# Weights loaded as fp32 in the same DMA row as q, k and v and cast by GpSimd, and batch 0 in another order, in a retention layer with a cosine-gated MLP

## The chip, the cores and the metric

The kernel runs on one core of a Trainium2 chip. The metric is device time in microseconds, the median of several runs of the whole program. A separate execution is profiled; all lines of traces are from it.

## What is computed

Inputs are q, k and v, each 8 batches x 8 heads x 576 positions x 64 (fp32), w_in (512 x 2048) and w_out (2048 x 512), fp32 too. The reference, cut to what matters:

```python
def _attn_ref(q, k, v):
    scores = scale * np.matmul(q, k.transpose(0, 1, 3, 2))
    gamma = 1.0 - 2.0 ** (-5.0 - np.arange(H, dtype=np.float32))
    Dmat = np.where(rel >= 0, gamma[:, None, None] ** rel[None, :, :], 0.0)   # rel = row - column
    return np.matmul(scores * Dmat[None], v)
...
x = np.ascontiguousarray(attn_out.transpose(0, 2, 1, 3)).reshape(B * S, H * D)
h = x @ w_in
g = h * np.cos(h)
return g @ w_out
```

So it is causal attention without softmax and with a decay per head, and then an MLP of width 2048 on 4608 tokens, gated by the cosine of its own hidden values.

## The kernel before

**Retention.** Positions are taken in chunks of 128. q is scaled by gamma to the position, v by gamma to minus the position (`decay`, L371), so that inside a chunk only a mask of zeros and ones is left. `scores` makes k^T q of a chunk for all heads (PSUM, names `sc` or `mm`), and VectorE masks it into `rt`. `rest` adds past and own part of a chunk's output into a PSUM bank (`po` or `mm`): four matmuls with the state `sb` of the chunks before, eight with `rt` and the scaled v (`vb`). Its result is copied to `xt`, the transposed input of the MLP. `state_mm` adds k^T v of a chunk to the running state (`st` in PSUM), and `state_copy` copies that to `sb` in two instructions of ScalarE.

Batches 0 and 1 are done chunk by chunk. Of each, k and q of the first 512 positions come as four "quads" (`quad`, L322: rows of 4 positions of one head, pieces of 1 KB), are cast or scaled (`quad_cast`), transposed on TensorE (`quad_turn`) into `kqt`, and k is transposed back (`back`) into `kq`. The v of a chunk comes in pieces of 256 bytes (`load`, L299). The last 64 positions, chunk 4, are loaded the same way. From token 1152 on there are 27 groups of 128 tokens (g = 9 to 35), loaded by `load_g` (L305), scaled by GpSimd (`casts_g`) and transposed by a DMA on SP's queue (`turn_dma`, L388 to L390, writes `kqt`); `quarters` does their retention.

**MLP.** Tokens go in tiles of 512 (j = 0 to 8). `mlp1` makes one of 16 column groups of the hidden layer: four matmuls with `win` into a bank, a cosine on ScalarE (a sine with a shift, `cb`, L552), a product on VectorE (`gt`, L554). For j = 0 the 512 tokens of batch 0 are taken in two halves of 256 for the first four groups, (0, 256) from chunks 0 and 1 and (256, 256) from chunks 2 and 3. The product with `wout` is done plainly for j = 0 and 1 (`plain2`, four matmuls a step; for j = 0 step n takes the n//4-th quarter of w_out) and by a scheme of seven products after that, for which VectorE makes sums of w_out's blocks (`tsum`).

**Order.** Everything is emitted by one Python program (`emit`, L905) that puts each instruction behind the one before on its engine; waits come from a small scheduler that knows who wrote and read each buffer. Loads of q, k and v go to 16 fp32 buffers `ld` of 128 x 512 in turn (`fetch`, L285) by SP's DMA queue. They stand in a list, `pend`; `pump` (L883) issues from its front as many as have a buffer whose reader has been emitted, and holds groups back while too many buffers are in use. SP does its row in order, DMA transposes among it, each with the waits for its own buffer.

**The weights** come by DMAs that GpSimd issues (`w_in_load`, L327, and `w_out_load`, L332): eight, each a quarter of a matrix (1 MB of fp32), which the DMA itself casts to bf16 in `win` or `wout`. In GpSimd's row w_in's four stand between the scalings of batch 0's v, w_out's four behind them. An entry `after` in the list lets SP wait for the second piece of w_in before it fetches anything for batch 0's last chunk and batch 1.

Of the kernel before, what the change touches and what calls it, by code (L numbers as in the profile page):

```python
# [12 lines left out]
DFF = 2048  # L13
DM = H_ * D_
# [39 lines left out]
class Tok:  # L54
    __slots__ = ("eng", "sem", "val", "clock", "seq")
    n = 0
# [87 lines left out]
class _Kernel:  # L144
# [182 lines left out]
    def w_in_load(self, g):  # L327
        dst = bass.AP(self.WIN, 512 * g, [[4 * DFF, 128], [DFF, 4], [1, 512]])
        src = bass.AP(self.w_in, 512 * g, [[DFF, 128], [128 * DFF, 4], [1, 512]])
        self.wtok[f"wi{g}"] = self.s.dma("pool", f"wi{g}", lambda e: e.dma_start(dst, src), writes=[self.bWIN[g]])  # L330

    def w_out_load(self, g):  # L332
        dst = bass.AP(self.WOUT, 4 * g * DM, [[16 * DM, 128], [DM, 4], [1, DM]])
        src = bass.AP(self.w_out, 4 * g * 128 * DM, [[DM, 128], [128 * DM, 4], [1, DM]])
        w = Buf()
        t = self.s.dma("pool", f"wo{g}", lambda e: e.dma_start(dst, src), writes=[w])
        for i in range(4 * g, 4 * g + 4):
            self.bWOUT[i].w = [t]
        self.wtok[f"wo{g}"] = t
# [543 lines left out]
    def pump(self):  # L883

        while self.pend:
            fn, a = self.pend[0]
            if fn == self.after:
                if a[0] not in self.wtok:
                    return
            else:  # L890
                n = 3 if fn == self.load_g or fn == self.load and len(a) == 2 else 1
# [13 lines left out]
    def emit(self):  # L905
# [3 lines left out]
        for b in range(2):  # L909
            if b:  # L910
                self.push(self.after, "wi1")
                self.push(self.load, 0, 4)
            for c in range(NP):
                for x in "kq":
                    self.push(self.quad, x, b, c)
            for r in range(4):
                self.push(self.load, b, r, "v")
        self.push(self.load, 1, 4)
# [24 lines left out]
        for r in range(4):  # L943
            self.w_out_load(r)
# [21 lines left out]
        m1(range(2), (0, 256))  # L966
        self.rest(0, 3, state=False)
        m1(range(2, 4), (0, 256))
# [7 lines left out]
        self.casts(0, 4)  # L976
        self.pump()
# [9 lines left out]
        for n in range(16):  # L987
# [119 lines left out]
```

## Time and profile before

| | us |
|---|---|
| median of 3 runs (298.09 to 298.13) | 298.09 |
| profiled execution, its own time | 299.12 |
| span of its instructions | 297.4 |
| TensorE busy | 285.3 |
| VectorE busy | 214.6 |
| ScalarE busy | 173.9 |
| GpSimd busy | 95.6 |

HBM was read for 36.70 MB and written for 9.44 MB. The granted TensorE clock was 1.00 all through. Times in traces count from the start of the span. In a timeline a row gives start, length, engine, line, operation, output<-input, shape and count, and in brackets the idle time of the engine ahead of it and what ended that; SPq is SP's DMA queue. "Busy" of TensorE includes the pipelining of matmuls, and a few matmul records are missing, so that "x2" stands for three here and there. In the chain of waits each row is a piece of the chain that ended last: start, length, who.

### The profile page before, as it was taken

To read this page: it belongs to the slowest core of one execution; us is meant where nothing else is said; L and a number is where in the kernel's file an instruction comes from. 1 tells how busy PE (TensorE), PEld (TensorE's weight loads), DVE (VectorE), ACT (ScalarE), POOL (GpSimd) and SP (SyncE) were. 2 spreads that over 40 slices of the span, in tenths; PEclk is the share of its full clock that TensorE was granted. 3 is DMA by queue.
4 is the path that set the end of the run, shared out by engine and by line. 5 is a ranking of instruction groups with operands and counts; after the bars stand their busy time and mean duration, and the time that the engine had idled before them with its cause. 6 is when DMAs were issued, how large, how long until landed. Compare 5 with 4: busy or idle time off the path is not lost.

```text
span 297.4 us, 8336 instructions
## 1 busy us (share of the span) xinstructions
PE 285.3 (96%) x3526; PEld 180.6 (61%) x3558; DVE 214.6 (72%) x465; ACT 173.9 (58%) x344; POOL 95.6 (32%) x120
## 2 busy tenths in 40 slices
PE   6899999999998999999999999999999999999996
PEld 2465455655553568646864785478547854785485
DVE  3667848568567688579857985798579757956973
ACT  6688624797347664566457535753586358535720
POOL 3580237754426430580058006700670030000000
PEclk9999999999999999999999999999999999999999
DMA  6999999999999999999999965899591170013013
GB/s 202 230 200 193 197 330 182 270 228 181 210 227 236 186 202 215 251 203 182 207 237 224 197 150 145 174 228 166 153 200 5 37 143 3 2 36 108 0 37 106
DMA packets 142325, 49.70 MB, mean 167 GB/s; under 512 B 125904, under 2 KB 141264, under 8 KB 142288
## 3 DMA queue, kind: packets, MB, share of 16 engines
q1 hardware_dynamic: 129280, 35.53, 67.3%
q10 hardware_dynamic: 8784, 9.44, 9.9%
q0 software_dynamic: 4224, 4.19, 8.7%
q8 instruction: 28, 0.46, 0.7%
q14 instruction: 9, 0.07, 0.1%
HBM read 36.70 MB, written 9.44 MB: 155 GB/s over the span
## 4 chain that ended last, share of the span: by engine, by line
PE 84%; DMA 9%; issue 2%; SPq 2%; DVE 1%; ACT 1%; DVEq 0%
PE mm L461 56%; PE mm L463 19%; DMA ld<-in_q_dram 3%; PE st L709 3%; PE sc L709 2%; DMA win<-in_moe_w_in_dram 2%; DMA ld<-in_v_dram 2%; DMA kqt<-kq 2%; SPq L290 2%; PE po L709 2%; PE sc L461 1%; PE po L461 1%; PE st L461 0%; PE sc L463 0%; ACT cb L552 0%
## 5 line engine op out<-in xcount | busy, mean ns | idle before, releaser
L554 DVE TENSOR_TENSOR gt<-mm,cb 128x512 bf16<-128x512 f32 (+3 forms) x156 | 99.4, 647 | 35.0 <-ACT cb L552 34.0
L552 ACT ACTIVATE cb<-mm,c_pih 128x512 bf16<-128x512 f32 (+3 forms) x156 | 100.7, 654 | 37.3 <-PE mm L463 36.4
L461 PE MATMUL mm<-xt,win 128*128 128x512 bf16 (+3 forms) x446 | 113.4, 362 | 3.1 <-issue 1.9
L461 PEld LDWEIGHTS mm<-xt,win 128*128 128x128 bf16 x468 | 43.5, 98 | 45.2 <-DVE gt L554 0.8
L463 PE MATMUL mm<-xt,win 128*128 128x512 bf16 (+3 forms) x156 | 56.6, 363 | 0.1
L342 POOL CAST kq<-ld 128x512 bf16<-128x512 f32 (+1 forms) x29 | 17.7, 610 | 117.4 <-PE mm L463 100.6
L461 PE MATMUL mm<-wout,gt 128*128 128x256 bf16 (+1 forms) x256 | 49.1, 309 | 1.0 <-issue 0.8
L461 PE MATMUL mm<-ts,ss 128*128 128x256 bf16 x240 | 35.4, 273 | 0.0
L461 PEld LDWEIGHTS mm<-wout,gt 128*128 128x128 bf16 x264 | 24.7, 98 | 11.8 <-DVE gt L554 0.5
L342 ACT ACTIVATE u<-mm 128x512 f32<-128x512 f32 x21 | 12.5, 597 | 32.3 <-PE mm L463 32.3
L365 POOL TENSOR_TENSOR vb<-ld,wv 128x512 bf16<-128x512 f32 x27 | 28.4, 1052 | 6.4 <-DMA ld<-in_v_dram 4.0
L361 POOL TENSOR_TENSOR kq<-ld,uq 128x512 bf16<-128x512 f32 x27 | 28.2, 1044 | 4.3 <-DMA ld<-in_q_dram 4.3
L342 ACT ACTIVATE xt<-po 128x256 bf16<-128x256 f32 (+1 forms) x35 | 14.6, 418 | 23.0 <-PE st L709 15.7
L463 PE MATMUL mm<-wout,gt 128*128 128x256 bf16 (+1 forms) x88 | 27.4, 311 | 0.1
L643 DVE TENSOR_TENSOR osb<-mm,u 128x512 f32<-128x512 f32 x20 | 13.8, 688 | 18.8 <-PE mm L463 11.2
L750 DVE TENSOR_TENSOR rt<-sc,mh 128x256 bf16<-128x256 f32 x54 | 21.2, 416 | 5.9 <-PE st L709 2.5
L463 PEld LDWEIGHTS mm<-xt,win 128*128 128x128 bf16 x156 | 15.3, 98 | 16.0
L461 PEld LDWEIGHTS mm<-ts,ss 128*128 128x128 bf16 x240 | 23.0, 98 | 2.8
L463 PE MATMUL mm<-ts,ss 128*128 128x256 bf16 x80 | 21.8, 272 | 0.0
L576 DVE TENSOR_TENSOR ss<-gt 128x512 bf16<-128x512 bf16 x56 | 20.7, 417 | 0.0
L760 DVE TENSOR_TENSOR pf<-sc,pf 128x256 f32<-128x256 f32 x42 | 17.6, 420 | 1.1
L709 PE MATMUL po<-rt,vb 64*64 64x64 bf16 x216 | 13.4, 202 | 0.1
(154 smaller groups left out, 386.6 us busy)
## 6 DMA issues: line engine op xcount, KB each, us to landing
out_dram<-osb ACTq DMA_DIRECT2D x35, 256.0 KB, 3.5
ld<-in_k_dram SPq DMA_DIRECT2D x32, 256.0 KB, 4.8
ld<-in_q_dram SPq DMA_DIRECT2D x32, 256.0 KB, 5.1
ld<-in_v_dram SPq DMA_DIRECT2D x32, 256.0 KB, 5.7
win<-in_moe_w_in_dram POOLq DMA_DIRECT2D x4, 512.0 KB, 10.2
wout<-in_moe_w_out_dram POOLq DMA_DIRECT2D x4, 512.0 KB, 17.0
ld<-in_k_dram SPq DMA_DIRECT2D x8, 128.0 KB, 4.5
ld<-in_q_dram SPq DMA_DIRECT2D x8, 128.0 KB, 4.0
```

The lines of the kernel that those rows point to most:

```text
L342: fn = (lambda e: e.activation(o, x, AF.Copy)) if eng == "act" else (lambda e: e.tensor_copy(o, x))
L361: self.s.op("pool", lambda e: e.tensor_tensor(o, a, w, ALU.mult), reads=[bt, self.bUQ], writes=[self.bQB[i]])
L365: self.s.op("pool", lambda e: e.tensor_tensor(o2, a2, w2, ALU.mult), reads=[bt, self.bWV], writes=[self.bVB[i]])
L461: self.nc.tensor.matmul(o, a, b, **kw)
L463: return s.done("pe", self.nc.tensor.matmul(o, a, b, **kw), reads, writes)
L552: s.op("act", lambda e: e.activation(ci, mi, AF.Sin, bias=self.C_PIH.ap(), scale=1.0), reads=[bm, self.bC], writes=[self.bCB[i]])
L554: s.op("dve", lambda e: e.tensor_tensor(bass.AP(self.GT, dt * TB + o0, [[16 * TB, 128], [1, n]]), mi, ci, ALU.mult), reads=[bm, self.bCB[i ...
L576: self.s.op("dve", lambda e: e.tensor_tensor(self.s_(k, d), a, b, op), reads=rd, writes=[S[k - 1][p]])
L643: self.s.op("dve", lambda e: e.tensor_tensor(o, m, x, ALU.add), reads=[bm, self.bU[u]], writes=[self.bOSB[i]])
L709: inst = self.nc.tensor.matmul(o, a, c, **kw)
L750: s.op("dve", lambda e: e.tensor_tensor(bass.AP(self.RT[n % 2][x], 0, p3), bass.AP(self.SC[x], 0, p3), bass.AP(self.MH, 0, [[64, 128], [0, ...
L760: s.op("dve", lambda e: e.tensor_tensor(self.PF[t].ap(), u, self.PF[1 - t].ap(), ALU.add), reads=[self.bSU[t], self.bPF[1 - t]], writes=[s ...
```

## The change

1. The weights are fetched by SP as fp32, into the same 16 buffers as q, k and v: 32 fetches of 128 x 512 (256 KB, rows of 2 KB), four to a piece (`w_load`). GpSimd casts each into `win` or `wout` (`w_cast`, 32 instructions). GpSimd issues no DMA any more, and SP's wait for w_in's second piece is gone.
2. The list has w_in's first piece ahead of batch 0's fourth v, the other three and two pieces of w_out behind it, and w_out's last two around batch 1's quads.
3. Batch 0 is emitted in another order: chunk 1's output earlier and copied by ScalarE instead of VectorE, the first MLP groups ahead of chunk 2's state and output, the fourth v scaled by VectorE instead of GpSimd, and two pairs of idle matmuls (which only fill waits) left out.

The core of the diff:

```diff
+    def w_load(self, x, g):
+        for c in range(4):
+            if x == "in":
+                src = bass.AP(self.w_in, 128 * c * DFF + 512 * g, [[DFF, 128], [1, 512]])
+            else:
+                src = bass.AP(self.w_out, (4 * g + c) * 128 * DM, [[DM, 128], [1, DM]])
+            self.fetch((x, g, c), src, [[1, DM]], 128)
+
+    def w_cast(self, eng, x, g, cs=range(4)):
+        for c in cs:
+            t, bt = self.use((x, g, c))
...
+            u = self.copy(eng, o, t.ap(), [bt], [Buf()])
+            (self.bWIN[g] if x == "in" else self.bWOUT[4 * g + c]).w.append(u)
...
+        quads(0)
+        vs(0, range(3))
+        ws("in", [0])
+        vs(0, [3])
+        ws("in", range(1, 4))
+        ws("out", range(2))
+        self.push(self.load, 0, 4)
+        ws("out", [2])
+        quads(1)
+        ws("out", [3])
+        vs(1, range(4))
         self.push(self.load, 1, 4)
...
-        self.s.need("pool", [self.wtok["v", 0, 0]])
-        self.w_in_load(0)
         self.decay("dve", "v", 0, 0)
-        self.w_in_load(1)
-        for r in range(1, 4):
+        for r in range(1, 3):
             self.decay("pool", "v", 0, r)
-            if r < 3:
-                self.w_in_load(r + 1)
-        for r in range(4):
-            self.w_out_load(r)
+        self.w_cast("pool", "in", 0)
...
         self.scores(0, 2)
+        self.rest(0, 1, self.bank(), state=False)
         self.back(0, 2, "act")
-        self.idle(2)
         self.state_mm(0, 1)
-        self.rest(0, 1, self.bank(), "dve", False)
         self.state_copy(1)
         self.scores(0, 3, False)
-        self.idle(2)
+        self.decay("dve", "v", 0, 3)
+        m1(range(2), (0, 256))
+        for g in range(1, 4):
+            self.w_cast("pool", "in", g)
+            self.pump()
+        for g in range(2):
+            self.w_cast("pool", "out", g)
+            self.pump()
         self.state_mm(0, 2)
         self.state_copy(2)
         self.rest(0, 2, state=False)
-        m1(range(2), (0, 256))
-        self.rest(0, 3, state=False)
-        m1(range(2, 4), (0, 256))
+        m1(range(2, 3), (0, 256))
+        self.rest(0, 3, self.bank(), state=False)
+        m1(range(3, 4), (0, 256))
         m1(range(3), (256, 256))
...
         self.casts(0, 4)
+        self.w_cast("pool", "out", 2)
...
+            if n == 9:
+                self.w_cast("pool", "out", 3)
+                self.pump()
```

Three places in the rows of the engines. First SP's DMA row behind batch 0's quads, before the change (128x8x64 is a v of 128 positions, 64x8x64 a chunk 4, 128x2x256 a quad):

```order
L290 DMA ld<-in_v_dram 128x8x64 x4
L290 DMA ld<-in_k_dram 64x8x64
L290 DMA ld<-in_q_dram 64x8x64
L290 DMA ld<-in_v_dram 64x8x64
L290 DMA ld<-in_k_dram 128x2x256
L290 DMA ld<-in_q_dram 128x2x256
```

and of the change, from the same place:

```order
L290 DMA ld<-in_v_dram 128x8x64 x3
L290 DMA ld<-in_moe_w_in_dram 128x512 x4
L290 DMA ld<-in_v_dram 128x8x64
L290 DMA ld<-in_moe_w_in_dram 128x512 x12
L290 DMA ld<-in_moe_w_out_dram 128x512 x8
L290 DMA ld<-in_k_dram 64x8x64
L290 DMA ld<-in_q_dram 64x8x64
L290 DMA ld<-in_v_dram 64x8x64
L290 DMA ld<-in_moe_w_out_dram 128x512 x4
L290 DMA ld<-in_k_dram 128x2x256
```

The weights' 32 fetches, of which the last four stand behind batch 1's quads, are now in one row with the rest; from batch 1's v on, the row has the same loads and transposes in the same order as before.

Second, GpSimd behind batch 0's four casts of k, before the change:

```order
L330 DMA win<-in_moe_w_in_dram 128x4x512 x2
L378 TENSOR_TENSOR vb<-ld,wv 128x512
L330 DMA win<-in_moe_w_in_dram 128x4x512
L378 TENSOR_TENSOR vb<-ld,wv 128x512
L330 DMA win<-in_moe_w_in_dram 128x4x512
L378 TENSOR_TENSOR vb<-ld,wv 128x512
L336 DMA wout<-in_moe_w_out_dram 128x4x512 x4
L342 COPY kq<-ld 64x512
```

and of the change (the copies into win and wout are the casts):

```order
L381 TENSOR_TENSOR vb<-ld,wv 128x512 x2
L345 COPY win<-ld 128x512 x16
L345 COPY wout<-ld 128x512 x8
L345 COPY kq<-ld 64x512
L381 TENSOR_TENSOR kq<-ld,uq 64x512
L381 TENSOR_TENSOR vb<-ld,wv 64x512
L345 COPY wout<-ld 128x512 x4
L345 COPY qs<-ld 128x2x4x64 x4
L345 COPY wout<-ld 128x512 x4
```

The issues of weight DMAs ahead of the v are gone, the fourth v too, and the casts stand ahead of batch 0's chunk 4, of batch 1's quads and of batch 1's v.

Third, ScalarE from batch 0's first state copies (sb) to the cosines (cb) of the second 256 tokens, before the change:

```order
L342 ACTIVATE sb<-st 64x4x64 x2
L342 ACTIVATE xt<-po 128x4x128
L342 ACTIVATE kq<-mm 128x512
L342 ACTIVATE sb<-st 64x4x64 x4
L342 ACTIVATE xt<-po 128x4x128
L552 ACTIVATE cb<-mm,c_pih 128x256 x2
L342 ACTIVATE xt<-po 128x4x128
L552 ACTIVATE cb<-mm,c_pih 128x256 x5
```

and of the change:

```order
L345 ACTIVATE sb<-st 64x4x64 x2
L345 ACTIVATE xt<-po 128x4x128
L345 ACTIVATE xt<-mm 128x4x128
L345 ACTIVATE kq<-mm 128x512
L345 ACTIVATE sb<-st 64x4x64 x2
L555 ACTIVATE cb<-mm,c_pih 128x256 x2
L345 ACTIVATE sb<-st 64x4x64 x2
L345 ACTIVATE xt<-po 128x4x128
L555 ACTIVATE cb<-mm,c_pih 128x256
L345 ACTIVATE xt<-mm 128x4x128
L555 ACTIVATE cb<-mm,c_pih 128x256 x4
```

Chunk 1's output (xt<-mm) has come to ScalarE, and the third pair of state copies and chunk 2's output now stand behind the first two cosines.

More of the change, by code (lines that the diff above doesn't have):

```diff
@@ L325, in quad @@
         self.fetch((x, b, "c", c), src, [[4 * D_, 2], [1, 4 * D_]], 128)
[L327 to L339, printed above, removed]
+    def w_load(self, x, g):
[8 more added lines that the diff above has]
+            t, bt = self.use((x, g, c))
+            o = (bass.AP(self.WIN, c * DFF + 512 * g, [[4 * DFF, 128], [1, 512]]) if x == "in"
+                 else bass.AP(self.WOUT, (4 * g + c) * DM, [[16 * DM, 128], [1, DM]]))
+            u = self.copy(eng, o, t.ap(), [bt], [Buf()])
+            (self.bWIN[g] if x == "in" else self.bWOUT[4 * g + c]).w.append(u)
     def copy(self, eng, o, x, reads, writes):
@@ L886, in pump @@
             fn, a = self.pend[0]
[L887 to L891, printed above, removed]
+            if True:
+                n = 4 if fn == self.w_load else 3 if fn == self.load_g or fn == self.load and len(a) == 2 else 1
                 if any(self.busy[(self.n_ld + i) % NL] for i in range(n)):
@@ L908, in emit, with quads @@
         self.busy = [False] * NL
[L909 to L912, printed above, removed]
+        def quads(b):
             for c in range(NP):
@@ L915, in emit, with vs, ws @@
                     self.push(self.quad, x, b, c)
-            for r in range(4):
+        def vs(b, rs):
+            for r in rs:
                 self.push(self.load, b, r, "v")
+        def ws(x, gs):
+            for g in gs:
+                self.push(self.w_load, x, g)
+        quads(0)
[9 more added lines that the diff above has]
+        vs(1, range(4))
         self.push(self.load, 1, 4)
@@ L934, in emit @@
                 self.idle(2 if c else 1)
-        self.s.need("pool", [self.wtok["v", 0, 0]])
-        self.w_in_load(0)
         self.decay("dve", "v", 0, 0)
-        self.w_in_load(1)
-        for r in range(1, 4):
+        for r in range(1, 3):
             self.decay("pool", "v", 0, r)
-            if r < 3:
-                self.w_in_load(r + 1)
-        for r in range(4):
-            self.w_out_load(r)
+        self.w_cast("pool", "in", 0)
         self.pump()
```

## The prediction

> **What bounds the kernel now.** I read the page's busy line first, then the busy time by stage, cut at the two places where the chain of work that ended last leaves TensorE.
>
> ```profile
> span 297.4 us, 8336 instructions
> PE 285.3 (96%) x3526; PEld 180.6 (61%) x3558; DVE 214.6 (72%) x465; ACT 173.9 (58%) x344; POOL 95.6 (32%) x120
> ```
>
> ```profile
> 0.00:19.10 19.10, 15.40 (x160) 7.79 (x162) 10.93 (x33) 12.61 (x25) 10.73 (x22) 1.00 0.93 211
> 19.10:95.20 76.10, 74.06 (x761) 40.37 (x773) 50.99 (x102) 48.32 (x97) 33.82 (x41) 1.00 1.19 224
> 95.20:96.70 1.50, 0.25 (x13) 0.14 (x12) 1.32 (x2) 0.69 (x1) 1.50 (x2) 1.00 1.25 234
> 96.70:297.40 200.70, 195.58 (x2601) 132.34 (x2620) 151.39 (x329) 112.24 (x222) 49.52 (x58) 1.00 0.74 141
> ```
>
> The columns are the stretch, its length, busy time of PE, PEld, DVE, ACT and POOL, granted clock, DMA share, GB/s. From 19.1 us on TensorE is busy all the time at full clock but for 95.2 to 96.7. So only two things can move the end: when the MLP's matmuls start, and that hole. The chain of waits names what ended each:
>
> ```profile
> 12.01 7.08 DMA win<-in_moe_w_in_dram
> ...
> 19.14 0.50 PE mm L461 x3
> ```
>
> ```profile
> 91.10 5.54 DMA kqt<-kq
> ...
> 96.68 0.32 PE sc L709 x16
> ```
>
> ```profile
> 96.68 0.32 PE L709 MATMUL sc<-kqt 64*64 64x64 bf16 x16 [1.25 <-DMA kqt<-kq]
> ```
>
> First w_in's first piece, issued at 12.01 and landed 7.08 later, at 19.09; then the DMA transpose of group 13, issued at 91.10 and landed at 96.64, for which TensorE stood **1.25 us**. Why it is late stands in SP's queue in order of time:
>
> ```profile
> 4.88 6.61 SPq L290 DMA_DIRECT2D ld<-in_v_dram  x4
> 22.73 0.72 SPq L290 DMA_DIRECT2D ld<-in_k_dram  x1
> ...
> 49.80 0.62 SPq L317 DMA_DIRECT2D ld<-in_k_dram  x1
> ...
> 88.45 2.61 SPq L317 DMA_DIRECT2D ld<-in_v_dram  x1
> 91.10 2.84 SPq L390 DMA_TRANSPOSE kqt<-kq  x1
> ...
> 96.32 2.23 SPq L390 DMA_TRANSPOSE kqt<-kq  x1
> ```
>
> SP stands from 11.5 to 22.7 for w_in's second piece. From 49.80 (group 9) to 91.10 the listing has 28 rows with under 0.1 us between any two, most longer than the 0.62 us of a free issue: the queue is pushed back by the transfers in front of it. What reaches SP earlier at 49.8 should bring that transpose earlier by as much.
>
> **The change, part by part.** (a) **The start.** Now the first piece lands in four fetches behind v's third chunk, and GpSimd casts it.
>
> ```profile
> 8.43 0.62 POOL L342 CAST qs<-ld 128x512 bf16<-128x512 f32 x1 [0.84 <-DMA ld<-in_k_dram]
> ...
> 10.71 0.69 DVE L416 TENSOR_TENSOR qs<-ld,uq 128x512 bf16<-128x512 f32 x1 [0.85 <-DMA ld<-in_q_dram]
> ...
> 11.72 0.69 DVE L378 TENSOR_TENSOR vb<-ld,wv 128x512 bf16<-128x512 f32 x1 [0.33 <-DMA ld<-in_v_dram]
> ...
> 13.70 1.06 POOL L378 TENSOR_TENSOR vb<-ld,wv 128x512 bf16<-128x512 f32 x1
> ```
>
> The first v lands 1.01 us after the last q; at that pace the second and third land at 12.75 and 13.75. GpSimd, which no longer issues two weight DMAs ahead of 13.70, scales them (1.06 each) until 13.8 and 14.9, then makes four casts of 0.61 (the row at 8.43): **17.3**, since the last fetch, 0.7 us apart from 13.75 on, is there at 16.5. That is 1.7 us ahead of 19.09. But ScalarE's new order now sets the pace, by these rows of before:
>
> ```profile
> 14.62 0.78 ACT L342 ACTIVATE sb<-st 64x256 bf16<-64x256 f32 x2
> ...
> 15.43 0.60 ACT L342 ACTIVATE xt<-po 128x512 bf16<-128x512 f32 x1
> ...
> 15.92 0.59 ACT L342 ACTIVATE kq<-mm 128x512 bf16<-128x512 f32 x1
> ...
> 16.30 0.40 PE L461 MATMUL mm<-kqt,sb 128*128 128x128 bf16 x4
> ...
> 16.83 0.22 PE L463 MATMUL mm<-rt,vb 128*64 128x128 bf16 x1
> ...
> 19.79 0.91 ACT L552 ACTIVATE cb<-mm,c_pih 128x256 bf16<-128x256 f32 x2 [0.18 <-PE mm L463]
> ...
> 21.57 0.49 PE L461 MATMUL mm<-xt,win 128*128 128x256 bf16 x3
> ```
>
> ScalarE takes 0.49 from start to start for 512 columns, 0.80 for a pair of state copies, 0.44 for a cosine of 256 columns. Chunk 1's output needs the state copies (end 15.4) and 0.75 on TensorE (16.30 to 17.05): 16.25. Then xt 16.3, kq 16.8, two sb 17.3, two cosines 18.1, two sb 19.0, xt 19.8, cosine 20.3, chunk 3's xt 20.75 to 21.35. That last one opens the second 256 tokens, where TensorE went without a stop before: 21.4 against 21.57. **The start gives 0.15 us**, not 1.7: the state copies and chunk 2, which before lay in the wait for w_in, now lie behind the first cosines. Each 0.1 us that w_in comes after 17.4 costs as much.
>
> (b) **The fetches.** SP's row is now one stream, with no wait for w_in and no second queue. I follow it to a mark that both kernels have, q of group 9:
>
> ```profile
> 46.81 0.69 DVE L416 TENSOR_TENSOR qs<-ld,uq 128x512 bf16<-128x512 f32 x1 [0.29 <-DMA ld<-in_q_dram]
> ...
> 50.98 1.04 POOL L378 TENSOR_TENSOR vb<-ld,wv 128x512 bf16<-128x512 f32 x1 [0.21 <-DMA ld<-in_v_dram]
> ...
> 55.55 1.04 POOL L361 TENSOR_TENSOR kq<-ld,uq 128x512 bf16<-128x512 f32 x1 [0.40 <-DMA ld<-in_q_dram]
> ```
>
> From batch 1's last q to group 9's q are 8.74 us, the same transfers in both kernels. A k or q by quads takes (10.71 - 8.43) / 3 = 0.76, a v 1.01, a half-size chunk 0.8 (4.57 us from 50.98 to 55.55, less two full loads at 1.06, by 3). So after: 10.71 + 4 x 1.01 + 3 x 0.8 + 8 x 0.76 + 8.74 = 31.97, and 32 weight fetches of 256 KB at p each. No row of before shows p, a load of 2 KB rows from SP. The nearest:
>
> ```profile
> 41.00:44.00 3.00, 2.84 (x31) 1.79 (x31) 1.08 (x3) 0.98 (x2) 0.62 (x1) 1.00 1.12 347
> 48.30:50.00 1.70, 1.62 (x17) 0.81 (x17) 1.11 (x3) 0.39 (x1) 1.62 (x3) 1.00 1.17 247
> ...
> 18.00:26.00 8.00, 7.56 (x84) 5.27 (x82) 4.87 (x11) 7.07 (x16) 3.36 (x5) 1.00 1.22 199
> ```
>
> The first is quads (pieces of 1 KB, 347 GB/s, 0.755 us for 256 KB), the second v (256 bytes, 247 GB/s, 1.06 us), the last the old weight DMAs alone: 199 GB/s counted as bf16, so 398 read, 0.66 us for 256 KB of fp32. A straight line through 1024 pieces at 1.06 and 256 at 0.755 gives 0.70 for 128. I take **p = 0.68**, between 0.66 and 0.70; the slow end is the quads' own 0.76, the fast end 0.66. Then q of group 9 is there at 31.97 + 21.76 = 53.7, **1.8 us earlier** (2.5 at 0.66, 1.2 at 0.70, 0.7 later at 0.76; break-even at 0.737). The transpose of group 13 moves from 96.64 to 94.8, and TensorE, which would come for it at 95.1 to 95.3, does not wait: **1.25 us**. Late next would be the transpose issued at 96.32. At 5.54 us from issue to landing, as the one before it, it is there at 101.9, and its scores begin behind this row:
>
> ```profile
> 102.60 0.15 PE st L709 x2
> ```
>
> With TensorE 1.4 earlier, at 101.2, and the transpose 1.8 earlier, at 100.1, it is in time. In general the gain is the smaller of the queue's lead and 1.4.
>
> (c) **The weights' due times.** Pieces are due at 4 of 16 matmul groups each:
>
> ```profile
> 24.92 0.82 PE L461 MATMUL mm<-xt,win 128*128 128x512 bf16 x3
> ...
> 34.43 0.81 PE L461 MATMUL mm<-wout,gt 128*128 128x512 bf16 x3
> ```
>
> The rows are group 5 of w_in and group 0 of w_out, 11 groups apart, so a group takes 0.865: the third w_in piece (group 8) is due at 27.5, the fourth at 31.0, w_out's first at 34.4. At p = 0.68 four fetches take 2.7 us: behind the fourth v (17.6) the second piece is cast by 21.0, the third 23.7, the fourth 26.4, w_out's first 29.2. At 0.76 it is 30.5 for the last. Covered by 4 us.
>
> (d) **GpSimd's 32 casts** are 32 x 0.61 = 19.5 us, less eight issues of about 0.8. Room is there:
>
> ```profile
> 19.10:34.40 15.30, 15.08 (x102) 8.57 (x105) 10.32 (x18) 13.18 (x24) 2.87 (x5) 1.00 1.22 196
> 34.40:55.60 21.20, 20.50 (x190) 10.71 (x192) 13.52 (x23) 8.56 (x18) 11.93 (x15) 1.00 1.11 242
> ```
>
> Some 20 casts (12.2 us) fall into the first stretch, with 12.4 us idle, eight (4.9) into the second, with 9.3 idle. I cost them at nothing. If w_out's last four casts ran late, batch 1's v chunks behind them on GpSimd, and the state matmuls that need these, would pay it one for one.
>
> (e) DVE gives up a copy and takes a v chunk, 0.69 each; the four idle matmuls taken out lay in waits. Nothing.
>
> Sum: 0.15 + 1.25 = **1.4 us** off the span of 297.4. The profiled execution took 299.12, 1.7 more than its span; the three runs' median of 298.09 is 0.7 more. I leave that remainder as it is: 298.09 - 1.4 = **296.7 us**.
>
> **The rivals.** *The weights flow no faster than the quads* (slower). At 0.76 per fetch the stream reaches group 9 at 56.3, 0.7 late; TensorE then waits at group 13 for the old 1.25, 0.7 more and its own 0.15: 298.8. It decides from p = 0.737 up. For it: those 0.76 are the only loads of large pieces by SP in the trace. Against: 398 GB/s read by the old weight DMAs, and 256-byte to 1 KB pieces gaining 100 GB/s.
>
> *All reads meet a ceiling near break-even* (no change). If fetches settle at 0.73 (359 GB/s, between the quads' 347 and the old weight DMAs' 398), the queue's lead is 0.2: 297.9. The 398 GB/s of the weights in 18 to 26 us speak against a ceiling so low. The Trainium skill, "DMA: Bandwidth & Descriptors", Specifications, has such a ceiling: about 358 GB/s of HBM per core, which as an estimate is 0.73 us for 256 KB. By that rule the time would be 297.9, by the rows 296.7; this case's trace, with 398 GB/s read, does not agree.
>
> *The start falls back.* If ScalarE's or GpSimd's chain ends 0.8 later than I add up (w_in at 18.2), the second 256 tokens start 0.65 after 21.57, and of 1.25 only 0.6 is left: 297.5. I added up 14 rows, each good to 0.05.
>
> *More is won.* If the front comes 0.7 earlier still and p is 0.66, both holes close: 296.0.
>
> **How the numbers follow.** Forecast 50% (its own range 296.2 to 297.4), slow weights 23%, ceiling 10%, start falls back 10%, more won 7%. A measurement of this kernel can tell about 0.2%, 0.6 us, from no change. Faster: 50 + 7 + half of the third rival, 62%; within 0.2%: the ceiling and the other half, 15%; slower: 23%. The range, 296.0 to 299.0, takes in both ends of p.
>
> **What would show it.** Right: q of group 9 cast near 53.7, no wait on kqt near 95, the second 256 tokens at 21.4 although w_in is ready by 17.4. Wrong: fetches of w_in more than 0.74 apart, casts on GpSimd that TensorE waits for, a wait on kqt of over 1.25 us.

## The result, and the profile after

The changed kernel takes 301.5 us (median of 4 runs, 301.26 to 302.25), the kernel before 298.11 beside it (298.09 to 299.93): ratio 1.0103, 95% interval 1.006 to 1.0145. It is **slower by 3.4 us**, some 1%. The profiled execution took 301.66. One run below, of e5 at 305.72 us, lay over 1.5% above the fastest of its kernel and is left out of e5's median and ratio.

The page of the changed kernel: its span, what was busy, and, in 40 slices of 7.5 us, the granted clock and the GB/s.

```profile
span 299.9 us, 8412 instructions
...
PE 289.3 (96%) x3554; PEld 180.8 (60%) x3554; DVE 217.3 (72%) x465; ACT 174.4 (58%) x345; POOL 108.8 (36%) x143
...
PEclk9999999999999799999999999999999999999999
...
GB/s 210 270 355 387 256 358 225 295 212 174 218 208 227 188 229 211 215 218 211 187 204 217 190 186 129 165 228 187 139 196 20 37 131 14 2 36 107 0 35 107
```

Two things stand out. The weights do flow: 355 and 387 GB/s in the third and fourth slice. And there is one slice, from 97.5 us on, whose clock is a 7. What TensorE waited for (total, times, longest):

```profile
PE sc L712 <- DMA kqt<-kq: 2.9, 1, 2.9
PE mm L464 <- POOL win L345: 1.5, 1, 1.5
```

The wait that was to vanish is 2.9 us in place of 1.25. In TensorE's order of time (start, duration, idle before and what ended it):

```profile
18.03 0.50 PE L464 MATMUL mm<-xt,win 128*128 128x256 bf16 x3 [1.48 <-POOL win L345]
...
21.91 0.49 PE L464 MATMUL mm<-xt,win 128*128 128x256 bf16 x3 [0.24 <-ACT xt L345]
...
97.89 0.43 PE L712 MATMUL sc<-kqt 64*64 64x64 bf16 x16 [2.94 <-DMA kqt<-kq]
...
105.13 0.30 PE L712 MATMUL sc<-kqt 64*64 64x64 bf16 x16
```

These are the first group of the MLP, the first of the second 256 tokens, and the scores of groups 13 and 14. From group 13's to group 14's are 7.24 us. The stretches around it show why:

```profile
87.90:94.80 6.90, 6.90 (x100) 3.37 (x97) 4.79 (x12) 4.81 (x9) 2.91 (x4) 1.00 1.25 256
94.80:97.80 3.00, 0.15 (x8) 0.04 (x6) 1.25 (x2) 0.69 (x1) 2.28 (x3) 0.93 1.04 154
97.80:101.20 3.40, 3.31 (x55) 1.77 (x56) 0.00 (x0) 0.49 (x1) 1.06 (x3) 0.56 1.33 246
101.20:105.10 3.90, 3.90 (x24) 1.62 (x24) 3.63 (x8) 3.52 (x8) 1.75 (x2) 1.00 1.17 146
```

TensorE is full until 94.8, stands for 3 us, and then works for 3.4 us at a granted clock near **one half** (0.56 in this cut). The trace's clock record has the change at 97.38 and the return at 100.80. This is not the profiled execution's alone: 3.4 us at one half in a span of 300 make a mean clock of 0.994, and the four runs of the changed kernel show 0.994, 0.989, 0.994 and 0.994.

**Against a second execution of before.** The kernel before was profiled once more (e9 below: 297.48 us, span 295.8). Its rows for the same three places, without the first:

```profile
20.74 0.49 PE L461 MATMUL mm<-xt,win 128*128 128x256 bf16 x3
...
95.02 0.32 PE L709 MATMUL sc<-kqt 64*64 64x64 bf16 x16 [1.21 <-DMA kqt<-kq]
...
100.96 0.30 PE L709 MATMUL sc<-kqt 64*64 64x64 bf16 x16
```

So against this execution the changed kernel is 21.91 - 20.74 = **1.17** late at the second 256 tokens, 97.89 - 95.02 = 2.87 at group 13 (**1.70** more: 2.94 waited in place of 1.21), 105.13 - 100.96 = 4.17 at group 14 (**1.30** more, the half clock), and the span is 4.1 longer. Three terms, and nothing behind 105. (Against the first profile of before, whose w_in landed only at 19.09, the start's term is 0.34.)

### The profile page after: what moved, and what is told of

Its sections match the earlier page's. It is cut to its first block, busy times and chain, and to the rows that moved or that the text cites. A ratio compares the mean times of both kernels' runs of the same rounds, so it can differ in the third digit from the quotient of the medians.

```text
span 299.9 us, 8412 instructions
## 1 busy us (share of the span) xinstructions
PE 289.3 (96%) x3554; PEld 180.8 (60%) x3554; DVE 217.3 (72%) x465; ACT 174.4 (58%) x345; POOL 108.8 (36%) x143
## 4 chain that ended last, share of the span: by engine, by line
PE 76%; DMA 13%; SPq 6%; POOL 2%; ACT 1%; issue 1%; DVE 0%; POOLq 0%; DVEq 0%
PE mm L464 51%; PE mm L466 17%; DMA ld<-in_k_dram 6%; DMA ld<-in_q_dram 4%; SPq L290 3%; PE st L712 2%; PE sc L712 2%; DMA ld<-in_moe_w_in_dram 2%; DMA kqt<-kq 2%; PE po L712 1%; SPq L317 1%; PE sc L464 1%; SPq L393 1%; POOL kq L345 1%; PE sc L466 1%
## 5 line engine op out<-in xcount | busy, mean ns | idle before, releaser
L464 PE MATMUL mm<-xt,win 128*128 128x512 bf16 (+3 forms) x468 | 119.2, 365 | 2.1 <-POOL win L345 1.5
L466 PE MATMUL mm<-xt,win 128*128 128x512 bf16 (+3 forms) x156 | 56.8, 364 | 0.0
L464 PE MATMUL mm<-wout,gt 128*128 128x256 bf16 (+1 forms) x264 | 50.9, 312 | 0.0
L646 DVE TENSOR_TENSOR osb<-mm,u 128x512 f32<-128x512 f32 x20 | 13.8, 688 | 18.8 <-PE mm L466 11.2
L466 PE MATMUL mm<-wout,gt 128*128 128x256 bf16 (+1 forms) x88 | 27.4, 311 | 0.0
L345 ACT ACTIVATE xt<-po 128x256 bf16<-128x256 f32 (+1 forms) x34 | 14.0, 413 | 22.9 <-PE st L712 15.7
```

The costliest lines, as they stand in the source:

```text
L345: fn = (lambda e: e.activation(o, x, AF.Copy)) if eng == "act" else (lambda e: e.tensor_copy(o, x))
L464: self.nc.tensor.matmul(o, a, b, **kw)
L466: return s.done("pe", self.nc.tensor.matmul(o, a, b, **kw), reads, writes)
L646: self.s.op("dve", lambda e: e.tensor_tensor(o, m, x, ALU.add), reads=[bm, self.bU[u]], writes=[self.bOSB[i]])
```

## The experiments

A number in bold is the median of a kernel's runs, its range behind it; ratios are against the kernel before on the same chip (medians 297.88, 297.89 and 298.2). "T-early" is one constant of the row's planning: how far the loads of a group may run ahead of it. Each kernel has one profiled execution. Those of e1, e5 and e7 are the fastest of their runs (297.99, 299.73 and 295.8), so what made the other runs slower stands in no trace. Some code cuts below join several lines into one.

### Is it the transpose? e1 and e2

In the changed kernel (e1) and the kernel before (e2), the loads of groups 16 to 19 are held back until a later step, so SP issues the transposes of groups 13 to 16 one group of loads earlier:

```diff
-if fn == self.load_g and sum(self.busy) + n > (AHEAD if a[0] < 4 * 4 else AHEAD + 3):
+if fn == self.load_g and sum(self.busy) + n > (AHEAD if a[0] < 20 else AHEAD + 3):
```

> The change, with one constant altered: groups 16 to 19 are held back like the groups before them, so that SP issues the DMA transposes of groups 13 to 16 one group of loads earlier in its row. My theory now: nearly all of the loss comes at one place, the scores of group 13, where TensorE stood 2.94 us for that transpose (1.25 before) and then ran at a clock of 0.5 for some 3.4 us. If so, both vanish here, the 0.44 us that TensorE was ahead at the scores of group 12 stay, and the time is 296.0 to 297.0, faster than both kernels. Rival: the stream of loads is late as a whole, and the wait comes back at a later transpose: 299 to 301.

> The kernel before, with the same constant altered. My theory: the only wait of TensorE behind the start, 1.25 us at group 13, vanishes and nothing follows it: 296.7 to 297.2. If the transposes are merely moved against loads that are then late themselves, it stays at 298.1 or gets slower.

e1: **299.69** us (297.99 to 301.79), ratio to before 1.006 (1.0025 to 1.0095). e2: **297.48** (297.10 to 298.31), 0.9983 (0.9957 to 1.0008). In both profiles the wait at group 13 is gone, and no half clock is left ahead of the very end. For e1 that is some 1.8 us less than the changed kernel: wait and half clock together are about half of the loss, not all, and the share is not sharp, since the two intervals overlap. Its runs are 3.8 us apart with a mean clock of 1.0 in nine of ten, so what spreads them is not the half clock. e2 gained 0.4 where 1.25 had been waited, and its interval takes in no change at all. In its trace, group 15 to 16 takes 115.54 - 108.76 = 6.78 us, 0.7 more than the 115.62 - 109.53 = 6.09 of e9; with this row among them:

```profile
110.74 0.50 PE L461 MATMUL mm<-ts,ss 128*128 128x256 bf16 x3 [0.27 <-DVE ss L576]
```

More than half of what was saved came back two groups later.

### Does standing still cost clock? e3, e5 and e6

e3 puts idle matmuls on zeros ahead of group 13's scores in the changed kernel, which change no transfer; e5 has them too, and six more ahead of the MLP's first group; e6 has those six and T-early.

```diff
+        self.idle(6)                     # e5, e6
         m1(range(2), (0, 256))
...
+                    if j == 2 and dt == 4:
+                        self.idle(12)    # e3, e5
                     self.visit(g + dt // 6)
```

> The change, with 12 idle matmuls (0.22 us each, 2.6 us together) ahead of the retention of group 12 in tile 2, where TensorE waits for the transpose of group 13. They fill the wait and end before the transpose has landed. If the half clock behind the wait is caused by TensorE standing still, the clock stays at 1.00 and the time is 1.2 to 1.5 us less, some 300.2. If it has another cause, the half clock is still there and the time is 301.3 or more.

> The kernel after, with six idle matmuls (1.3 us) ahead of the first group of the MLP, where TensorE stands 1.48 us for w_in's first piece, and twelve (2.56 us) ahead of group 13's scores, where it stands 2.94. No transfer is changed. Theory (two prices: the wait itself, and a stretch of 3.4 us at half clock when TensorE has stood still before it): half clock at no place but the very end, the wait's time stays (nothing is done in it), the end 1.3 earlier than after: 300.2 us (299.8 to 300.6). Rival (the half clock is not set off by standing still): half clock at 20 or at 98 as before, 301.5 and no change against the kernel after.

> The kernel after with the six idle matmuls at the start and with groups 16 to 19 held back (the constant of the first experiment), so no transpose is waited for. Theory (what spread the first experiment's runs between 298.0 and 301.8 is the half clock at the start, after TensorE stood 1.5 us there): no half clock in the first 30 us, all runs within 0.5 of each other, 297.7 us (297.3 to 298.3). Rival (the spread comes from elsewhere, from the transposes or the queue): median 299.7 as in the first experiment, with a spread of 3 us.

e3: **301.51** (300.46 to 302.84), ratio 1.0109 (1.0073 to 1.0144): no gain, a miss. Four of its six runs show a mean clock of 1.0 and still took 300.46 to 301.61. In its profile the idle matmuls ran until 99.05, half a us longer than the wait, whose transpose landed at 98.57; so they cost time themselves. The half clock at 98 is gone there, but one is there at the start, where TensorE stood 1.72 us for w_in:

```profile
15.60:19.00 3.40, 1.68 (x34) 1.21 (x29) 2.08 (x4) 1.72 (x4) 2.11 (x4) 1.00 0.97 278
19.00:22.40 3.40, 3.40 (x33) 2.19 (x30) 1.31 (x3) 2.36 (x6) 1.95 (x4) 0.50 1.04 386
```

TensorE was busy for 1.68 of 3.40 us, and the next 3.4 us ran at 0.50. With both gaps filled (e5) the profile has no half clock, and group 14 follows group 13 as fast as in before:

```profile
97.14 0.30 PE L712 MATMUL sc<-kqt 64*64 64x64 bf16 x16
...
103.27 0.32 PE L712 MATMUL sc<-kqt 64*64 64x64 bf16 x16
```

6.13 us in place of 7.24, and a profiled time of 299.73; the wait itself stays, filled with zeros. (This execution is 1.9 us faster than the changed kernel's; 1.1 of that is the half clock, the other 0.75 a transpose that landed earlier, with group 13 at 97.14 in place of 97.89.) That the half clock is set off by standing still is shown by the traces. In the medians about half of it comes out, and not clear of noise: e5 **300.79** (299.73 to 301.67), 1.0083 (1.005 to 1.0117), though all its runs show a clock of 1.0. And e6, with nothing to wait for at group 13 and the start filled, took **300.4** (299.39 to 301.64), 1.0087 (1.0051 to 1.0122), where 297.7 was expected. So the spread of e1 is not the half clock at the start: that idea falls. e6's profile names what else is late:

```profile
PE mm L464 <- POOL wout L345: 0.9, 1, 0.9
PE mm L464 <- ACT xt L345: 0.8, 2, 0.6
```

The first, at 49.77, is w_out's late fetches, from the new row. Of the second, 0.24 lie at the start, and 0.59 at 112.22, near the place where T-early gave time back in e2.

### What makes the row late? e4, e8 and e10

The row of the changed kernel is read best on GpSimd, which takes each load as it lands:

```profile
12.49 2.04 POOL L381 TENSOR_TENSOR vb<-ld,wv 128x512 bf16<-128x512 f32 x2 [2.62 <-DMA ld<-in_v_dram]
15.24 2.73 POOL L345 CAST win<-ld 128x512 bf16<-128x512 f32 x4 [0.71 <-DMA ld<-in_moe_w_in_dram]
19.97 8.07 POOL L345 CAST win<-ld 128x512 bf16<-128x512 f32 x12 [2.00 <-DMA ld<-in_moe_w_in_dram]
...
31.77 0.61 POOL L345 CAST wout<-ld 128x512 bf16<-128x512 f32 x1 [0.35 <-DMA ld<-in_moe_w_out_dram]
32.67 0.61 POOL L345 CAST wout<-ld 128x512 bf16<-128x512 f32 x1 [0.29 <-DMA ld<-in_moe_w_out_dram]
33.72 0.61 POOL L345 CAST wout<-ld 128x512 bf16<-128x512 f32 x1 [0.44 <-DMA ld<-in_moe_w_out_dram]
34.73 0.61 POOL L345 CAST kq<-ld 64x512 bf16<-64x512 f32 x1 [0.40 <-DMA ld<-in_k_dram]
...
57.74 1.04 POOL L364 TENSOR_TENSOR kq<-ld,uq 128x512 bf16<-128x512 f32 x1 [1.11 <-DMA ld<-in_q_dram]
```

and by stretches of the same execution (last column GB/s):

```profile
12.40:15.20 2.80, 2.25 (x42) 1.43 (x38) 2.80 (x5) 2.26 (x5) 2.04 (x2) 1.00 0.94 282
...
20.00:30.00 10.00, 9.76 (x74) 5.43 (x75) 5.71 (x12) 8.65 (x18) 9.10 (x15) 1.00 1.06 391
30.70:36.50 5.80, 5.80 (x29) 2.62 (x27) 4.77 (x8) 4.08 (x6) 3.86 (x7) 1.00 1.18 225
...
48.60:52.20 3.60, 3.60 (x47) 1.86 (x42) 2.92 (x5) 2.44 (x5) 3.13 (x4) 1.00 1.02 219
```

Among themselves the weights flow at 391 GB/s, 0.67 us per 256 KB. But w_in's first fetch lands at 15.18, 2.0 behind the third v; the next after the fourth v at 19.92, 1.75 behind it; the last three fetches of w_out ahead of the half-size chunks, and these, land 0.84 to 1.05 apart (31.71 to 36.50); and from 48.6 the v flow at 219 GB/s. q of group 9 is cast at 57.74; in e9 it is cast at 54.35:

```profile
54.35 1.04 POOL L361 TENSOR_TENSOR kq<-ld,uq 128x512 bf16<-128x512 f32 x1
```

But q of group 9 is a poorer mark than the forecast took it for. In the changed kernel two stores of results, issued by ScalarE, land between k and q of that group:

```profile
52.15 0.38 ACTq L874 DMA_DIRECT2D out_dram<-osb  x1
...
52.61 0.40 ACTq L874 DMA_DIRECT2D out_dram<-osb  x1
```

k lands at 55.41, the stores at 56.11 and 57.35, q at 57.67, 2.26 behind k. In the first profile of before and in e9 the first store lands behind q, and q is 1.19 and 0.72 behind k. At k, at 55.41 against 54.29 and 53.41, the row is 1.1 and 2.0 late. It stays so: the transposes up to group 13's land 0.8 to 2.1 later than in the first profile of before and 2.8 to 3.9 later than in e9.

e4 moves the fourth v ahead of w_in's first piece, so rows of 256 bytes and of 2 KB alternate once less; e8 puts w_out in one piece behind w_in, ahead of the half-size chunks and the quads, which also takes alternations away; e10 gives w_out to GpSimd's queue as before, issued behind the casts of w_in.

```diff
-        vs(0, range(3)); ws("in", [0]); vs(0, [3])
+        vs(0, range(4)); ws("in", [0])                          # e4
...
-        ws("out", range(2)); self.push(self.load, 0, 4); ws("out", [2]); quads(1); ws("out", [3])
+        ws("out", range(4)); self.push(self.load, 0, 4); quads(1)   # e8
+        self.push(self.load, 0, 4); quads(1)                        # e10, and w_out_load(0..3) on GpSimd
```

> The change, with w_in's first piece behind batch 0's fourth v and not ahead of it: one change from 256-byte rows to 2 KB rows less in SP's row. In the change the first fetch of 2 KB rows behind a v landed 2.0 us (behind the third v) and 1.75 us (behind the fourth) after the one before, against 0.68 from one to the next. If each such change costs 1.1 us, q of group 9 comes 1 us earlier here, TensorE's wait at group 13 is 1 us shorter, and the time is 0.5 to 2 us less (less still if the half clock goes). If what is slow is the start of the weights alone, wherever it stands, the stream is no earlier, w_in is cast 0.9 us later, and the time is the same or 0.5 us more.

> The kernel after with all of w_out in one piece of the row: w_in 1 to 3, w_out 0 to 3, the three half-size chunks, the quads, the v chunks (before: w_out 2 behind the half-size chunks and w_out 3 behind the quads); the casts of w_out 2 and 3 moved up likewise. The same bytes in the same queue, with three switches between row sizes fewer. Theory (the steady pace of 0.68 per 256 KB is as forecast, each switch to 2-KB rows behind shorter ones costs about 1 us, and the half-size chunks slow the weights beside them): q of group 9 at 56.0 in place of 57.7, the wait at group 13 1.2 in place of 2.9, no half clock there, the end 299.0 (298.4 to 300.2). Rival (the lateness is the pace of all the bytes, wherever they stand): q of group 9 at 57.7, wait 2.9, 301.5.

> The kernel after with w_out's four pieces sent by GpSimd's queue as DMAs that cast, as in the kernel before, issued behind the casts of w_in's third and fourth piece; w_in stays in SP's row. The same bytes are read, by two queues. Theory (one row has nothing to fill the gaps that it leaves where 2-KB rows follow 256-byte ones and where the half-size chunks lie among the weights): q of group 9 at 55 to 56 in place of 57.7, the wait at group 13 at most 1.3, no half clock there, 298.5 us (297.8 to 299.8). Rival (the bytes in front of group 9 are what counts, by however many queues): q of group 9 at 57.7, 2.9 waited, 301.5.

e4: **301.92** (301.62 to 303.44), 1.0131 (1.0081 to 1.0182). TensorE stood 3.36 us for w_in, 6.83 us of half clock followed. The row gained nothing by the alternation saved: the six fetches behind the third v (the fourth v and five of w_in) took 6.96 us here and 6.73 in the changed kernel, and q of group 9 landed 0.3 earlier where 1 was forecast.

e8: **304.15** (302.22 to 305.76), 1.0204 (1.0142 to 1.0265), worse, and by neither theory. Rows of its stretches, and of TensorE:

```profile
30.00:36.60 6.60, 6.55 (x32) 3.00 (x31) 5.40 (x9) 4.43 (x7) 6.10 (x10) 1.00 1.06 383
36.60:43.20 6.60, 1.96 (x14) 0.76 (x13) 1.05 (x2) 0.38 (x1) 4.28 (x8) 1.00 1.21 226
43.20:48.60 5.40, 5.24 (x37) 2.34 (x39) 2.62 (x6) 0.59 (x2) 2.05 (x3) 0.68 1.13 297
```

```profile
41.53 0.26 PE L464 MATMUL po<-ident,kq 64*128 64x64 bf16 x3 [3.31 <-POOL kq L345]
```

The end was lost because chunk 4, now behind all the weights, kept TensorE standing for 3.3 us, and half clock followed. For the row's pace only the landings count: from the fourth v to the last of weights and quads pass 29.80 us here (18.82 to 48.62), 29.85 in the changed kernel (18.17 to 48.02). And q of group 9 landed at 58.06, near the 57.7 of the rival. The fewer alternations gave **nothing**, so a fixed price per alternation is refuted. The changed kernel's own row says the same: w_out's fetch behind the half-size chunks landed 0.46 behind them, the one behind the quads 0.66. What is slow stays slow wherever it is put: the three half-size chunks and the weights beside them, 226 GB/s here at 36.6 to 43.2 and 225 there.

e10: **299.37** (298.52 to 301.37), 1.0063 (1.004 to 1.0087). The same bytes by two queues:

```profile
96.43 0.32 PE L721 MATMUL sc<-kqt 64*64 64x64 bf16 x16 [0.82 <-DMA kqt<-kq]
```

```profile
56.69 1.04 POOL L373 TENSOR_TENSOR kq<-ld,uq 128x512 bf16<-128x512 f32 x1
```

The wait is 0.82, with no half clock in this execution (four of the ten runs show one, with a mean clock of 0.994 or less). The kernel is 2.1 us faster than the changed one, within what was expected, though the two intervals overlap. But the theory behind it, that a second queue uses the time that one row leaves in its slow places, is **not shown**: q of group 9 is cast 1.05 earlier, but here no store lands ahead of it, and at k of group 9 the row is no earlier than the changed kernel's (55.63 against 55.41), nor at the first two transposes (67.46 and 68.71 against 67.42 and 68.67). The lead begins at the third, at 73.52 against 75.24, over 20 us behind the last weights, and what makes it is open.

e10 speaks to one more rival. SP must wait for buffers that GpSimd's casts empty; in the changed kernel's first 60 us it stood 11.2 us for casts of w_out and 3.6 for casts of w_in. If that made the row late, e10, which has no casts of w_out, should have been earlier at k of group 9, and was not. No run takes w_in's casts away as well.

### The start: e7, e9, e12 and e13

e7 is the kernel before without the two pairs of idle matmuls that the change removes; e9 is the kernel before, unchanged; e12 is the kernel before with w_in's first piece in SP's row, as in the change, and T-early; e13 is the changed kernel with that piece on GpSimd's queue again and batch 0 in its old order.

```diff
-        self.idle(2)                                            # e7, twice
...
-        self.w_in_load(0)
+        vs(0, range(3)); ws("in", [0]); vs(0, [3]); self.w_cast("pool", "in", 0)   # e12
...
-        vs(0, range(3)); ws("in", [0]); vs(0, [3]); ws("in", range(1, 4))
+        vs(0, range(4)); ws("in", range(1, 4)); self.w_in_load(0)                  # e13
```

> The kernel before without the two pairs of idle matmuls in batch 0 that the change takes out (0.85 us of matmuls on zeros). The forecast's step (e) gives them nothing: 298.1 (297.8 to 298.4). Theory (half clock after standing still): TensorE then stands about 1.6 us before w_in's first piece at 19.1; in some or all runs half clock for 3.4 us from about 20, which costs up to 1.7, so 298.1 to 299.8, median near 299.3, and runs further apart than the kernel before's.

> The kernel before, unchanged, profiled once more. The forecast took 1.25 us for TensorE's wait at group 13 from one profiled execution, which was 1.0 above the median of its runs. Theory (that wait is mostly the run's own, since the stream of loads shifts by some us from run to run): another wait at group 13 than 1.25, 0 to 0.6 in a run near 297.9. Rival (the wait is a fixture of the kernel before): 1.0 to 1.5 again.

> The kernel before (its order of batch 0, its casting DMAs) with one part of the change alone: w_in's first piece in SP's row ahead of the fourth v and cast by GpSimd; and groups 16 to 19 held back. Theory (the part of the change that helps is w_in's first piece, ready near 17.8 in place of 17.6 to 19.1 over the runs; the rest of the row hurts): 297.0 us (296.4 to 297.7), no wait for a transpose. Rival (the start is bound by ScalarE's chain or by w_in's second piece, which is issued 2 us later now): 297.5 or above, as the kernel before with those groups held back.

> The kernel after with one part undone: w_in's first piece by GpSimd's casting DMA behind the first v, the fourth v right behind the third and batch 0 in its old order, as in the kernel before; the other 28 fetches of weights stay in SP's row, cast by GpSimd. Theory (the start lost 1.2 us against an ordinary run of before because the fourth v and the work behind it come late, whatever the order of batch 0): the second 256 tokens at 20.2 to 21.6 as in the kernel before. The row is four fetches shorter, its steady part unchanged: q of group 9 at 55.0 to 56.0, the wait at group 13 0.5 to 2, in part of the runs a half clock behind it: 299.0 us (298.0 to 300.2). Rival (the start was not worse than before's): second 256 tokens at 21.9, and 300 or above.

e7: **297.6** (295.8 to 300.04), 0.998 (0.9947 to 1.0012). The idle matmuls are worth nothing that can be told from noise, as forecast. Its first MLP group starts at 17.65, 1.5 ahead of the first profile's 19.14 in a program that differs by four matmuls. And its profile has no wait at group 13: the transpose landed at 91.75, and the scores follow the matmul before them:

```profile
93.19 0.30 PE L709 MATMUL sc<-kqt 64*64 64x64 bf16 x16
```

e9: 297.48 in its one run. The wait at group 13 is 1.21 again, so it was not the first execution's own. A fixture it is not either: e7's execution, 1.7 us faster, is without it. w_in's first piece landed at 17.41 here and at 19.09 in the first profile, 1.7 us apart in two executions of one program.

e12: **297.71** (297.25 to 298.84), 0.9998 (0.9976 to 1.0019): no better than before, although nothing waits at group 13.

```profile
20.55 0.40 PE L478 MATMUL po<-kqt,sb 128*128 128x128 bf16 x4 [1.28 <-POOL vb L395]
...
22.11 0.49 PE L478 MATMUL mm<-xt,win 128*128 128x256 bf16 x3
```

```profile
17.94 1.49 POOL L330 DMA_DIRECT2D win<-in_moe_w_in_dram  x2
19.43 1.06 POOL L395 TENSOR_TENSOR vb<-ld,wv 128x512 bf16<-128x512 f32 x1
```

The MLP starts at 18.23, as in e9 (18.21), but the fourth v holds up chunk 3, and the second 256 tokens begin at 22.11 in place of 20.74. That v, now behind w_in's first piece, landed at 18.07 and was scaled only from 19.43, since GpSimd's issue of two more weight DMAs stood ahead of it; so 1.4 us of its lateness are this experiment's own. The changed kernel avoids that wait by its new order of batch 0, and pays as much: TensorE stands 1.48 ahead of 18.03, and the work that filled this time in before follows later (from there to the second 256 tokens 3.88 us, in e9 2.53).

e13: **302.12** (301.36 to 303.65), 1.0142 (1.0105 to 1.0179). Neither theory:

```profile
21.73 0.82 PE L469 MATMUL mm<-xt,win 128*128 128x256 bf16 x3 [3.75 <-DMA win<-in_moe_w_in_dram]
```

```profile
16.10:19.50 3.40, 1.89 (x34) 1.02 (x30) 1.89 (x3) 1.60 (x4) 1.22 (x2) 1.00 1.12 262
19.50:26.30 6.80, 4.57 (x29) 3.20 (x30) 1.02 (x3) 2.02 (x4) 4.36 (x8) 0.50 1.05 393
```

The first piece, issued at 11.34, landed at 21.7, over 10 us later, with SP's fetches of the second piece landing beside it; then 6.8 us at half clock. In the kernel before SP holds its row until w_in's second piece has landed, and there the first piece takes 5.5 to 7.1 us (e7, the first profile). So the hold seems to be what keeps that piece fast. The forecast had read it only as a loss for SP.

### Towards a faster kernel: e11, e14 and e15

e11 is e10 with T-early, e14 is e13 with T-early, and e15 is the kernel before with groups 16 and 17 alone held back:

```diff
-(AHEAD if a[0] < 4 * 4 else AHEAD + 3)
+(AHEAD if a[0] < 18 else AHEAD + 3)
```

> The same with groups 16 to 19 held back, so that the transposes of groups 13 to 16 are issued earlier. Theory: no wait for a transpose, no half clock, and w_out no longer comes late on GpSimd: 297.5 us (296.9 to 298.3). Rival (the spread of the first experiment, 298.0 to 301.8, comes from w_in's casts or the new order of batch 0): median 299.7 again.

> The same with groups 16 to 19 held back. Theory: no wait at group 13, a start as in the kernel before; what is left against it are GpSimd's casts of w_out, which come late by up to 1 us in some runs: 297.7 us (297.0 to 298.8). Rival (GpSimd's 28 casts and SP's longer row hurt elsewhere, as in the two-queue kernel that stayed at 299.6): 299.5.

> The kernel before with only groups 16 and 17 held back (the second experiment held 16 to 19, which took away the wait of 1.25 at group 13 and gave back 0.7 behind group 15, for DVE's ss). Theory: the wait at group 13 is gone, less is given back: 297.0 us (296.6 to 297.4), the fastest kernel here. Rival (every later transpose only moves the wait on): 297.5 to 298.0, no difference from before.

e11: **299.64** (298.35 to 301.34), 1.0058 (1.0033 to 1.0082). e14: **301.98** (301.65 to 302.69), 1.0132 (1.0095 to 1.0169). Both missed: with w_out, or w_in's first piece, in a second queue beside a full row, that piece comes late (1.1 us of waits for w_out in e11, 4.27 for w_in in e14). e15: **296.33** (296.07 to 296.87), 0.9947 (0.9928 to 0.9966), **faster than both kernels**:

```profile
span 294.6 us, 8368 instructions
```

```profile
93.73 0.30 PE L709 MATMUL sc<-kqt 64*64 64x64 bf16 x16
...
99.81 0.30 PE L709 MATMUL sc<-kqt 64*64 64x64 bf16 x16
```

No wait at group 13, and none given back: from group 15 to 16 are 114.47 - 108.38 = 6.09 us. Its span is 1.2 us below e9's, the size of the wait; the other 0.7 of the 1.9 in the medians is located in no trace.

## Why the prediction was wrong

It forecast 296.7 and faster; 301.5 was measured, outside its range.

- **Step (b) failed, in its sum.** "31.97, and 32 weight fetches of 256 KB at p each" with p = 0.68 put q of group 9 at 53.73; it landed at 57.67, 3.94 later. p was right: 0.67 to 0.68 wherever weights follow weights (391 GB/s, which also ends the rival of a ceiling at 359). Wrong was the rest, which took each kind of load at the pace it had among its like. By landings, in us over the forecast: third v -0.55 (this run's own); w_in's first piece and the fourth v, 4.98 in place of 3.73, +1.25; the next fetch, behind that v, +1.07; w_out's second piece from its second fetch on, with the half-size chunks and the fetch behind these, 6.21 in place of 5.12, +1.09; w_out's last piece +0.27; the remaining stretches of weights and quads -0.1. From there to k of group 9 it was right: 7.39, and 7.51 in the first profile of before. The last +1.07 is q, 2.26 behind k in place of 1.19: the step took "the same transfers in both kernels" for granted, and two stores of results landed in between. So the row itself was 2.9 late, and the mark added 1.1. e4 and e8 showed that the lateness is not a price per alternation. Why the fetches around a v and around the half-size chunks take longer together than the sum of their kinds was not measured and stays open.
- **What follows from a late row** was priced at the wait alone. The rival "the weights flow no faster than the quads" had the direction, and 298.8 for a lead of -0.7. Its mechanism was wrong (fetches are not 0.76 apart), and it lacked the second price: behind a stand of 2.94 us the clock halves for 3.4 us, 1.3 us more against e9 and 1.1 against e5, which shows that part by itself.
- **Step (a)** gave 0.15; the start lost 1.17 against e9. Second 256 tokens at 21.91 against a forecast of 21.4: 0.5 of it is mis-sized, since w_in was cast at 17.97, not 17.3, and the first group began at 18.03. The other 0.8 is the yardstick: 21.57 in the one profile of before, 20.74 and 20.18 in e9 and e7. In the profiles of kernels with before's start the first group of the MLP begins at 19.14 (the one used), 18.21 (e9), 17.65 (e7), 18.74 (e2) and 18.36 (e15): the run whose w_in landed latest was taken for the kernel.
- **The gain itself.** Even with the transposes in time, e2 kept only 0.4 of the 1.25 at group 13. The step "late next would be the transpose issued at 96.32" looked at transposes only; what came next, in e2, was a longer way from group 15 to 16, with the one wait named there on DVE. e15 gained 1.9, more than the wait, so there was something to win at this place; the rebuilt row was the wrong means.
- **Steps (c), (d), (e)** held in the profile of the changed kernel: no wait there for a cast but w_in's first; e7 shows no cost of the removed idle matmuls. TensorE's 1.48 us for that one cast are among the signs of being wrong that the forecast had named. Across runs (c) and (d) are less safe than the 4 us of cover said: e6 waited 0.9 for w_out.
- Not shown: the share of the start in the median. Start, wait and half clock add up in one pair of executions; the experiments that remove wait and half clock leave 1.8 to 2.5 of 3.4 us in the medians (e1, e6). The start is the only part of that located in both traces, at 0.7 (e1) and 0.9 us (e6) against e9; the rest stays open.

## What to carry to other kernels

A pace that a transfer has among its like is not its pace among others: where a change merges two queues, bound each mixed stretch from both sides, and ask which other transfers (here the stores of results) can land ahead of the mark. Before building on a wait, profile the kernel more than once: the landing of one DMA moved by 1.7 us between two executions of the same program, and the wait that the change was to remove was absent in e7's. And where the wait sits just behind a planning constant, try that constant first: one number (e15) won 1.9 us where a rebuilt row lost 3.4.

## What the runs showed of the hardware

- **Half clock behind a stand.** In these profiles every stretch of half clock but the one that the program's end cuts off is 3.41 or 6.83 us long, and the stretches of full clock between are multiples of it (13.65, 92.16, 293.55). So the clock seems to be decided once per 3.41 us, on a fixed grid. The length of a stand alone does not decide: 1.72 us in e3 was followed by half clock, 1.75 us in e2 (from 5.89) was not. Nor does TensorE's busy time in the 3.41 us before, where that is near one half. With 1.93 us of it, the changed kernel's start kept the full clock (first row), and e13 fell to half (second):

```profile
15.46:18.87 3.41, 1.93 (x36) 1.37 (x30) 2.51 (x4) 1.92 (x5) 2.23 (x4) 1.00 1.02 301
```

```profile
16.06:19.47 3.41, 1.93 (x36) 1.02 (x30) 1.89 (x3) 1.64 (x4) 1.22 (x2) 1.00 1.12 260
```

  Away from the program's end, half clock followed 0.36 (e8), 0.58 (e4), 0.98 (the changed kernel at 94), 1.63 (e14), 1.69 (e3) and 1.93 us of work (e13); full clock followed 1.71 (e2), 1.83 (e8) and 1.93. The Trainium skill, "TensorE: Matmul & The Clock Gate", Part 1, has a free-running window of 3413 ns and half rate after at least one idle window; the length agrees with these traces, but in e3 a window with 1.69 us of work in it was enough, well short of an idle one.
- **A casting DMA beside a row of fetches** took over 10 us from issue to landing (10.34 in e13, 10.89 in e14) where it took 5.54 (e7) to 7.08 (the first profile) with SP's row held.
